# Weight conversion in two slots per half unit, and key sums ahead of the products that read them

## The chip, the cores and the metric

The kernel runs on one core of a Trainium2 chip. The metric is device time in microseconds (us), the median of several runs; lower is better. The engines are TensorE (PE, with PEld for its weight loads), VectorE (DVE), ScalarE (ACT), GpSimd (POOL) and SyncE (SP, which here issues every transfer). Each engine works through its own queue in order: an instruction that waits for another engine holds up everything behind it in its queue.

## The reference

Three layers are computed one after the other, all in float32 accuracy:

```
attention, per batch (4) and head (8), 576 positions, head size 64
    phi(x) = [exp(x w - m), exp(-(x w - m))],  m = max |x w|   (128 + 128 features)
    kv = phi(k)^T v,   z = sum phi(k)
    out = (phi(q) kv) / (phi(q) z + 1e-6)
layer 1 (2304 tokens, 512 -> 2048 -> 512):  h = x w_in;  y = (h cos h) w_out
layer 2: a gate over 8 experts (softmax, then 8 rounds of row and column scaling),
    out = sum over experts of P[:, e] * (relu(x w1[e]) w2[e])    (512 -> 1024 -> 512)
```

The weights of layer 1, `w_in` and `w_out`, are float64. The kernel reads them as pairs of 32-bit words and makes float32 values of them itself.

## The kernel before

Products that need full accuracy are split: a value becomes a rounded high part (made by ACT, `act_hi`) and the rest as a low part (`dve_lo` on DVE or `pool_lo` on POOL), and a product takes three matmuls (`mm3`).

**Attention.** The 4 batches and 8 heads are worked in 16 pairs of heads. `attention()` (L331) is a software pipeline over `i` with three pairs in work at once: pair `i` is loaded, turned and projected, pair `i-1` gets its key sums, query features and the final products, and pair `i-2` is written out as input of layer 1. The string `ORDER` (L478) says in which order these steps are written within an iteration: `t` turns (transposes) queries or keys into tile `pa` and splits them to `Th`, `Tl`; `r` does the same for the remainder (`tr` is the turn, plain `r` its projection); `p` projects to `pp`, and DVE centres the result (`m`, then `u`); `c` is one of four pieces of the key sums `pk`, after the last of which ACT copies `kvz`; `f` turns `u` of the queries to `pu` and ACT takes the exponentials `qp`; `g` multiplies `qp` with `kvz` to `pn`, and DVE divides (`rd`, `xn`); `x` turns `xn` to `px` and `pz` and splits it to `xh`, `xl`; `k` advances the weight conversion by one slot. The exponentials of the keys, `kp`, are deferred by `KD` steps. PSUM tiles of the stage come from one pool of seven buffers, so a `pp` or `pu` can only be written when the tile seven before it has been read by ACT or DVE.

**Conversion.** `convert(f)` (L109) makes unit `f` of the layer 1 weights (16 units of two halves, so 32 halves). A half takes three slots: load the raw words (`raw`); mask, clamp and shift the high word on DVE (three operations on `cmag`) and take the low word to `csgn` on ACT; then on DVE put the sign in (`csgn`), on POOL add (`cmag`), on ACT round (`csp`, high part), on POOL subtract (`csp`, low part), and store to `wd`.

**Who sets the order.** What is written is not yet what stands in the queues: a scheduler takes the instructions, with the written order as priority, and places each on its engine's queue when its own model holds the engine free and the inputs ready. It moves conversion slots forward as far as buffers allow. The queues are then fixed; on the chip nothing is reordered.

After attention come layer 1 (`moe1_steps`, four blocks of 512 tokens and a rest of 256) and layer 2 over two passes and eight experts. Neither is touched by the change.

Of the kernel before, what the change touches and what calls it, by code (L numbers as in the profile page):

```python
# [9 lines left out]
F32 = mybir.dt.float32  # L10
F32R = mybir.dt.float32r
I32 = mybir.dt.int32
U32 = mybir.dt.uint32
AF = mybir.ActivationFunctionType
ALU = mybir.AluOpType
# [10 lines left out]
def kernel(ctx: ExitStack, tc: tile.TileContext, q, k, v, w_phi,  # L26
                         moe_w_in, moe_w_out, moe2_w_gate, moe2_w1, moe2_w2, out):
    nc = tc.nc
    B, H, S, D = q.shape
    NT, DM = out.shape  # L30
    DFF = moe_w_out.shape[0]
    NE, _, DF2 = moe2_w1.shape
    P = 128
    NP = H // 2
    KC = DM // P
    NF1 = DFF // P
# [27 lines left out]
    def pool_lo(lo, raw, hi):  # L64
        nc.gpsimd.tensor_tensor(out=lo, in0=raw, in1=hi.bitcast(F32), op=ALU.subtract)  # L65
# [4 lines left out]
    def act_hi(hi, raw):  # L70
        nc.scalar.copy(out=hi, in_=raw)  # L71
# [25 lines left out]
    vpool = ectx.enter_context(tc.tile_pool(name="vpool", bufs=2))  # L97
    apool = actx.enter_context(tc.tile_pool(name="apool", bufs=2, side="right"))
# [6 lines left out]
    wd = [dpool.tile([P, 2, 2, DM], F32, name=f"wd{f}") for f in range(NF1)]  # L105
    win32 = moe_w_in.bitcast(I32)
    wout32 = moe_w_out.bitcast(I32)

    def convert(f):  # L109
        for i in range(2):  # L110
            raw = vpool.tile([P, DM, 2], I32, name="raw64")
            if i == 0:
                nc.sync.dma_start(out=raw.rearrange("p (k f) t -> p k (f t)", k=KC),
                                  in_=win32[:, f * 2 * P:(f + 1) * 2 * P].rearrange("(k p) f -> p k f", p=P))
            else:
                nc.sync.dma_start(out=raw.rearrange("p f t -> p (f t)"), in_=wout32[f * P:(f + 1) * P, :])
            yield
            hw = raw[:, :, 1]
            lw = raw[:, :, 0].bitcast(U32)
            mag = vpool.tile([P, DM], I32, name="cmag", bufs=CB)  # L120
            sgn = vpool.tile([P, DM], I32, name="csgn", bufs=CB)
            nc.vector.tensor_scalar(out=mag, in0=hw, scalar1=2 ** 31 - 1, scalar2=None, op0=ALU.bitwise_and)
            nc.vector.tensor_scalar(out=mag.bitcast(F32), in0=mag.bitcast(F32), scalar1=2.0 ** -15, scalar2=None, op0=ALU.max)
            nc.vector.tensor_scalar(out=mag, in0=mag, scalar1=3, scalar2=None, op0=ALU.logical_shift_left)
            nc.scalar.activation(out=sgn.bitcast(F32), in_=lw, func=AF.Copy, scale=2.0 ** -51, bias=2.0)
            yield
            nc.vector.scalar_tensor_tensor(out=sgn, in0=hw, scalar=-2 ** 31, in1=sgn, op0=ALU.bitwise_and, op1=ALU.bitwise_or)
            nc.gpsimd.tensor_tensor(out=mag, in0=mag, in1=sgn, op=ALU.add)  # L128
            res = mag.bitcast(F32)
            sp = vpool.tile([P, 2, DM], F32R, name="csp")  # L130
            act_hi(sp[:, 0, :], res)
            pool_lo(sp[:, 1, :], res, sp[:, 0, :])
            nc.sync.dma_start(out=wd[f][:, i, :, :], in_=sp.bitcast(F32))
            yield

    vx_t = []
# [49 lines left out]
    def defer(n, fn):  # L186
        late.append([n, fn])
# [47 lines left out]
    def project_rem(st):  # L235
# [7 lines left out]
        st["kp"][2] = t  # L243
        defer(KD, lambda: exps((t[:, 0, :], t[:, 1, :]), u[:, 0, :]))
        yield 0.44

    def project(st, s, unit):
# [6 lines left out]
        if s == 0:  # L254
            t = apool.tile([P, 4, 2, P], F32, name="kp4")
            st["kp"][unit] = t
            defer(KD, lambda: exps((t[:, :, 0, :], t[:, :, 1, :]), u))
        else:
# [28 lines left out]
    def attend(st, unit):  # L287
        pn = apsum("pn")
        kvz, qp = st["kvz"], st["qp"][unit]
        if unit == 2:  # L290
            st["xn"] = apool.tile([P, 5, 2, D], F32, name="xn", bufs=XB)
            for a in range(2):
                for s in range(2):
                    nc.tensor.matmul(pn[0:D, a * P:(a + 1) * P], qp[:, s, a * D:(a + 1) * D], kvz[:, a, s, :],  # L294
                                     start=(s == 0), stop=(s == 1))
            pv = pn[0:D, 0:2 * P].rearrange("p (a c) -> p a c", a=2)
            xo = st["xn"][0:D, 4, :, :]
            n, pr = 2, D
        else:
            for j in range(4):  # L300
                for s in range(2):
                    nc.tensor.matmul(pn[:, j * P:(j + 1) * P], qp[:, s, j * P:(j + 1) * P], kvz[:, unit, s, :],  # L302
                                     start=(s == 0), stop=(s == 1))
            pv = pn.rearrange("p (j c) -> p j c", j=4)
            xo = st["xn"][:, 0:4, unit, :]
            n, pr = 4, P
        r = apool.tile([P, 4], F32, name="rd", bufs=4)[0:pr, 0:n]
        nc.vector.tensor_scalar(out=r, in0=pv[:, :, D], scalar1=1e-6, scalar2=None, op0=ALU.add)
        nc.vector.reciprocal(r, r)
        nc.vector.tensor_tensor(out=xo, in0=pv[:, :, 0:D], in1=r.unsqueeze(2).to_broadcast([pr, n, D]), op=ALU.mult)  # L310
        yield 0.44 * n
# [19 lines left out]
    def attention():  # L331
        nxt = load_heads(0, 0)
        work = {}
        for i in range(B * NP + 2):
            work = {0: nxt, 1: work.get(0), 2: work.get(1)}
            sums = key_sums(work[1]) if work[1] else None
            for step in ORDER.split():
                kind, arg = step[0], step[1:]
                st = work[0 if kind in "tprL" else 2 if kind == "x" else 1]
                if kind == "k":  # L340
                    if i < B * NP:
                        next(conv, None)
                elif st is None:
                    continue
                elif kind == "L":
                    nxt = load_heads(*divmod(i + 1, NP)) if i + 1 < B * NP else None
                elif kind == "c":
                    yield next(sums)
                elif kind == "t":
                    yield from turn_heads(st, arg)  # L350
                elif kind == "f":
                    yield from query_features(st, int(arg))
                elif kind == "r":
                    yield from project_rem(st)
                elif kind == "p":
                    yield from project(st, int(arg) // 2, int(arg) % 2)
                elif kind == "g":
                    yield from attend(st, int(arg))
                else:
                    yield from emit_x(st)  # L360
# [114 lines left out]
        defer(1, turn_logits)  # L475

    LAG = 2
    ORDER = "t0 c0 k t1 c1 x tr f0 c2 k p0 c3 L f1 p1 f2 r p2 g2 k p3 g0 k g1"  # L478
    XB = 1
    UB = 4  # L480
    KD = 1
    LD = 1
    MD = 1
    GD = 3
    CB = 2
# [28 lines left out]
    def pair_tile(b):  # L514
        pool = xpool2 if b < B - 1 else xpool
        return tuple(pool.tile([P, KC, MAIN], F32R, name=f"{n}{b}", bufs=1) for n in ("xh", "xl"))

    def conversion():
        for f in range(NF1):
            yield from convert(f)  # L520
            done_conv[0] = f + 1

    done_conv = [0]
    conv = conversion()
# [272 lines left out]
```

## Time and profile before

| | us |
| --- | --- |
| median of 3 runs (lowest to highest) | 2261.55 (2259.89 to 2261.65) |
| the profiled execution | 2266.37 |
| its span | 2264.6 |
| PE busy in it | 2200.8 (97%) |
| DVE busy | 1334.0 (59%) |
| POOL busy | 1070.0 (47%) |
| ACT busy | 966.1 (43%) |

The median is what a change is measured by; the profiled execution is where durations and waits are read. Times of rows are counted from the start of the span. A share of the whole span mixes stages with different limits: attention runs to about 310 us, where the last `pn` is done, and everything behind it is layer 1 and layer 2.

### The profile page before, as it was taken

Reading aid. Unit: us, or ns where it says so; the run is one execution under the profiler, and the core shown is the slowest. Engines: PE = TensorE matmul, PEld = TensorE weight load, DVE = VectorE, ACT = ScalarE, POOL = GpSimd, SP = SyncE. Lnnn points to the kernel's source line nnn. Section 1 sums busy time; section 2 is a strip of 40 time slices with the busy share of each in tenths; the row PEclk is TensorE's granted clock in tenths of the full one; section 3 lists DMA queues with packets and bytes.
Section 4 is the critical chain, followed back from the end, with each engine's and each line's share of the span. In section 5 each row is a group of like instructions: output and inputs, shape, how many; then the busy total and the mean of one; then the engine's idle time right before and its main releaser. Section 6 shows DMA issues by size and latency. Waiting matters only on the chain.

```text
span 2264.6 us, 33017 instructions
## 1 busy us (share of the span) xinstructions
PE 2200.8 (97%) x12853; PEld 1955.6 (86%) x12853; DVE 1334.0 (59%) x2498; ACT 966.1 (43%) x1565; POOL 1070.0 (47%) x704
## 2 busy tenths in 40 slices
PE   7988999999999999999999999989999999999999
PEld 7878888778787888999999999979999999999998
DVE  6879753333553886555555555685555555555555
ACT  4555555445554433343433434443433333343332
POOL 3324210000000566666675766755766757667562
PEclk8989999999999999999999999999999999999999
DMA  5766325555543211111111111131111111111111
GB/s 174 223 209 203 115 75 189 198 189 189 185 147 119 66 46 39 47 47 47 45 41 47 47 47 47 41 98 47 47 47 47 39 46 47 47 47 48 38 37 43
DMA packets 130956, 198.31 MB, mean 88 GB/s; under 512 B 33136, under 2 KB 87536, under 8 KB 130800
## 3 DMA queue, kind: packets, MB, share of 16 engines
q1 hardware_dynamic: 130800, 196.20, 26.7%
q8 instruction: 101, 1.65, 0.3%
q14 instruction: 55, 0.45, 0.1%
HBM read 169.95 MB, written 26.21 MB: 87 GB/s over the span
## 4 chain that ended last, share of the span: by engine, by line
PE 87%; DVE 5%; ACT 2%; DMA 1%; issue 1%; POOL 1%; SPq 0%; DVEq 0%; ACTq 0%; POOLq 0%
PE py L91 33%; PE pm L91 30%; PE ph L377 8%; PE acc L423 7%; PE pn L302 2%; PE pk L272 1%; PE pp L91 1%; PE acc L416 1%; POOL cmag L128 1%; PE pn L294 1%; DVE xcl L68 1%; DMA xs<-x2d 1%; PE ph L463 1%; POOL csp L65 0%; DMA raw<-in_moe_w_in_dram 0%
## 5 line engine op out<-in xcount | busy, mean ns | idle before, releaser
L704 DVE SCALAR_TENSOR_TENSOR acc<-py,logit,acc 128x512 f32<-128x512 f32 x531 | 398.3, 751 | 352.6 <-PE py L91 352.6
L91 PE MATMUL pm<-xch,w1h 128*128 128x288 f32 x1792 | 531.6, 297 | 4.4 <-DVE r L658 3.1
L91 PE MATMUL pm<-xch,w1l 128*128 128x288 f32 x1792 | 531.3, 297 | 0.0
L91 PE MATMUL pm<-xcl,w1h 128*128 128x288 f32 x1792 | 523.6, 292 | 0.0
L91 PE MATMUL py<-w2h,hh 128*128 128x512 f32 x1152 | 451.6, 392 | 7.4 <-DVE acc L704 3.9
L91 PE MATMUL py<-w2l,hh 128*128 128x512 f32 x1152 | 452.2, 393 | 0.0
L91 PE MATMUL py<-w2h,hl 128*128 128x512 f32 x1152 | 452.0, 392 | 0.0
L65 POOL TENSOR_TENSOR hl<-r,hh 128x1152 fp32r<-128x1152 f32 x128 | 345.5, 2699 | 87.4 <-ACT hh L71 86.8
L65 POOL TENSOR_TENSOR w2l<-raw,w2h 128x1024 fp32r<-128x1024 f32 x64 | 155.6, 2432 | 415.7 <-DMA xs<-x2d 409.6
L91 PEld LDWEIGHTS pm<-xch,w1h 128*128 128x128 f32 x1792 | 337.1, 188 | 11.9 <-DVE r L658 4.2
L91 PEld LDWEIGHTS pm<-xcl,w1h 128*128 128x128 f32 x1792 | 341.7, 191 | 4.9
L91 PEld LDWEIGHTS pm<-xch,w1l 128*128 128x128 f32 x1792 | 336.6, 188 | 0.1
L600 POOL TENSOR_TENSOR w1l<-raw,w1h 128x256 fp32r<-128x256 f32 x124 | 90.6, 752 | 438.3 <-ACT w1h L71 429.4
L678 ACT ACTIVATE r<-r 128x1152 f32<-128x1152 f32 x128 | 149.1, 1165 | 267.6 <-DVE r L658 255.2
L91 PEld LDWEIGHTS py<-w2h,hh 128*128 128x128 f32 x1152 | 217.2, 189 | 52.5 <-DVE acc L704 5.8
L91 PEld LDWEIGHTS py<-w2h,hl 128*128 128x128 f32 x1152 | 217.2, 189 | 46.3 <-POOL hl L65 0.3
L91 PEld LDWEIGHTS py<-w2l,hh 128*128 128x128 f32 x1152 | 217.3, 189 | 42.4
L654 ACT COPY keep<-pm 128x288 f32<-128x288 f32 x256 | 101.5, 398 | 338.4 <-PE pm L91 332.8
L658 DVE TENSOR_TENSOR r<-r,pm 128x288 f32<-128x288 f32 x512 | 215.9, 452 | 41.2 <-PE pm L91 40.9
L600 POOL TENSOR_TENSOR w1l<-ssum,w1h 128x1280 fp32r<-128x1280 f32 x62 | 183.9, 2966 | 2.7 <-ACT w1h L71 0.7
L658 DVE TENSOR_TENSOR r<-keep,pm 128x288 f32<-128x288 f32 x128 | 58.1, 454 | 202.6 <-PE pm L91 200.4
L377 PE MATMUL ph<-xh,wsp 128*128 128x512 f32 x512 | 171.8, 397 | 1.7 <-ACT hh L71 0.8
(163 smaller groups left out, 3311.4 us busy)
## 6 DMA issues: line engine op xcount, KB each, us to landing
wsp<-wd SPq DMA_DIRECT2D x128, 512.0 KB, 4.6
raw<-in_moe_w_dram SPq DMA_DIRECT2D x128, 512.0 KB, 3.5
wd<-csp SPq DMA_DIRECT2D x32, 512.0 KB, 3.3
raw<-in_moe_w_in_dram SPq DMA_DIRECT2D x16, 512.0 KB, 5.1
raw<-in_moe_w_out_dram SPq DMA_DIRECT2D x16, 512.0 KB, 5.1
kraw<-in_k_dram SPq DMA_DIRECT2D x16, 256.0 KB, 4.0
qraw<-in_q_dram SPq DMA_DIRECT2D x16, 256.0 KB, 3.1
vx<-in_v_dram SPq DMA_DIRECT2D x32, 128.0 KB, 2.8
```

The source lines that it names most:

```text
L65: nc.gpsimd.tensor_tensor(out=lo, in0=raw, in1=hi.bitcast(F32), op=ALU.subtract)
L68: nc.vector.tensor_tensor(out=lo, in0=raw, in1=hi.bitcast(F32), op=ALU.subtract)
L91: nc.tensor.matmul(ps, a, b, start=(i == 0), stop=(i == len(ops) - 1))
L128: nc.gpsimd.tensor_tensor(out=mag, in0=mag, in1=sgn, op=ALU.add)
L302: nc.tensor.matmul(pn[:, j * P:(j + 1) * P], qp[:, s, j * P:(j + 1) * P], kvz[:, unit, s, :], start=(s == 0), stop=(s == 1))
L377: nc.tensor.matmul(ph[:, 0:n], w, x, start=(i == 0), stop=(i == len(ops) - 1))
L423: nc.tensor.matmul(accs[blk][d], w[:, ds], g, start=(f == 0 and i == 0), stop=(f == NF1 - 1 and i == 2))
L600: eng.tensor_tensor(out=lo[:, sl], in0=src, in1=hi[:, sl].bitcast(F32), op=ALU.subtract)
L654: nc.scalar.copy(out=t, in_=ps[m])
L658: nc.vector.tensor_tensor(out=r[:, u, th, :], in0=r[:, u, th, :] if a is None else ps[a], in1=ps[b], op=op)
L678: nc.scalar.activation(out=rf, in_=rf, func=AF.Relu)
L704: nc.vector.scalar_tensor_tensor(out=a, in0=py, scalar=pe, in1=a, op0=ALU.mult, op1=ALU.add)
```

## The change

The conversion of a half takes two slots where it took three, and the slots of neighbouring halves overlap: in one slot ACT rounds the half before (`act_hi`), the next raw words are fetched, and DVE and ACT start on the present half; in the other slot DVE puts the sign in, POOL subtracts for the half before and adds for the present one, and the half before is stored. The string `ORDER` puts all four pieces of the key sums to the front of an iteration, projects between them and the products that read them, puts `g0` first among these and has three `k` steps where it had four; the first iteration has none. `KD` goes from 1 to 2, and the tile `xn` is taken at the first `attend` of a pair, whichever that is.

```diff
-    def convert(f):
-        for i in range(2):
-            raw = vpool.tile([P, DM, 2], I32, name="raw64")
...
+    def conversion():
+        n = 2 * NF1
+        raws, mags, sps = {}, {}, {}
+        def fetch(h):
...
+        fetch(0)
+        yield
+        for h in range(n + 1):
+            if h > 0:
+                sps[h - 1] = vpool.tile([P, 2, DM], F32R, name="csp")
+                act_hi(sps[h - 1][:, 0, :], mags[h - 1].bitcast(F32))
+            if h < n:
+                if h + 1 < n:
+                    fetch(h + 1)
+                hw = raws[h][:, :, 1]
...
+                nc.scalar.activation(out=sgn.bitcast(F32), in_=raws[h][:, :, 0].bitcast(U32), func=AF.Copy,
+                                     scale=2.0 ** -51, bias=2.0)
+                nc.vector.tensor_scalar(out=mag, in0=hw, scalar1=2 ** 31 - 1, scalar2=None, op0=ALU.bitwise_and)
+                nc.vector.tensor_scalar(out=mag.bitcast(F32), in0=mag.bitcast(F32), scalar1=2.0 ** -15, scalar2=None, op0=ALU.max)
+                nc.vector.tensor_scalar(out=mag, in0=mag, scalar1=3, scalar2=None, op0=ALU.logical_shift_left)
+                mags[h] = mag
             yield
...
-            nc.vector.scalar_tensor_tensor(out=sgn, in0=hw, scalar=-2 ** 31, in1=sgn, op0=ALU.bitwise_and, op1=ALU.bitwise_or)
-            nc.gpsimd.tensor_tensor(out=mag, in0=mag, in1=sgn, op=ALU.add)
-            res = mag.bitcast(F32)
-            sp = vpool.tile([P, 2, DM], F32R, name="csp")
-            act_hi(sp[:, 0, :], res)
-            pool_lo(sp[:, 1, :], res, sp[:, 0, :])
-            nc.sync.dma_start(out=wd[f][:, i, :, :], in_=sp.bitcast(F32))
+            if h < n:
+                nc.vector.scalar_tensor_tensor(out=sgn, in0=hw, scalar=-2 ** 31, in1=sgn, op0=ALU.bitwise_and, op1=ALU.bitwise_or)
+            if h > 0:
+                sp = sps.pop(h - 1)
+                pool_lo(sp[:, 1, :], mags.pop(h - 1).bitcast(F32), sp[:, 0, :])
+                nc.sync.dma_start(out=wd[(h - 1) // 2][:, (h - 1) % 2, :, :], in_=sp.bitcast(F32))
+                done_conv[0] = h // 2
+            if h < n:
+                nc.gpsimd.tensor_tensor(out=mag, in0=mag, in1=sgn, op=ALU.add)
             yield
@@ attend
+        if "xn" not in st:
+            st["xn"] = apool.tile([P, 5, 2, D], F32, name="xn", bufs=XB)
         if unit == 2:
-            st["xn"] = apool.tile([P, 5, 2, D], F32, name="xn", bufs=XB)
@@ attention
-                    if i < B * NP:
+                    if 0 < i < B * NP:
                         next(conv, None)
@@
-    ORDER = "t0 c0 k t1 c1 x tr f0 c2 k p0 c3 L f1 p1 f2 r p2 g2 k p3 g0 k g1"
+    ORDER = "t0 c0 k c1 t1 c2 k x c3 tr f0 f2 p0 L f1 p1 r p2 g0 p3 g2 g1 k"
-    KD = 1
+    KD = 2
```

What stands in the queues shows the change better than the written order. Line numbers of the changed kernel differ (there, L135 to L150 are the conversion, L249 and L250 the exponentials, L291 is `kvz`, L226 `Tr`). The first place is ACT's queue around the copy `kvz_2309` of one and the same pair of heads (the eleventh). Before:

```order
L71 CAST csp_3800<-cmag_3778 128x512
L125 ACTIVATE csgn_3930<-raw64_3900 128x512
L71 CAST csp_3882<-cmag_3847 128x512
L274 COPY kvz_2309<-pk_2310 128x512
L232 ACTIVATE qp4_2404<-pu_2399 128x512
L232 ACTIVATE kp4_2378<-u_2374 128x4x128
L233 ACTIVATE kp4_2378<-u_2374 128x4x128
L233 ACTIVATE qp4_2404<-pu_2399 128x512
L232 ACTIVATE qp1_2423<-pu_2421 128x128
L233 ACTIVATE qp1_2423<-pu_2421 128x128
```

Now:

```order
L71 CAST csp_3651<-cmag_3600 128x512
L71 CAST Th_2325<-pa_2327 128x512
L135 ACTIVATE csgn_3656<-raw64_3598 128x512
L71 CAST xh2_2137<-px_2349 128x512
L71 CAST x4h_120<-pz_2355 128x64
L291 COPY kvz_2309<-pk_2310 128x512
L226 COPY Tr_2366<-pr_2367 128x256
L249 ACTIVATE qp4_2376<-pu_2371 128x512
L250 ACTIVATE qp4_2376<-pu_2371 128x512
L249 ACTIVATE qp1_2381<-pu_2379 128x128
L250 ACTIVATE qp1_2381<-pu_2379 128x128
```

The rounding `csp` that stood right ahead of `kvz` now stands further up, ahead of a turn and of `xh`; the exponentials of the keys (`kp`) no longer stand between those of the queries (`qp`).

The second place is PE's queue at the start of the third iteration, from the turn of the keys on. Before:

```order
L218 MATMUL pa<-ident,kraw 128x128 x4
L270 MATMUL pk<-vx_115,kp_383 128x128
L272 MATMUL pk<-vx_115,kp_328 128x128 x4
L218 MATMUL pa<-ident,qraw 128x128 x4
L270 MATMUL pk<-vx_115,kp_383 128x128
L272 MATMUL pk<-vx_115,kp_328 128x128 x4
L319 MATMUL px<-ident,xn 128x128 x4
L324 MATMUL pz<-ident,xn 128x64
L208 MATMUL pr<-ident,kraw 128x128
L208 MATMUL pr<-ident,qraw 128x128
L281 MATMUL pu<-ident,u 128x128 x4
L270 MATMUL pk<-vx_115,kp_383 128x128
```

Now:

```order
L235 MATMUL pa<-ident,kraw 128x128 x4
L287 MATMUL pk<-vx_115,kp_363 128x128
L289 MATMUL pk<-vx_115,kp_321 128x128 x4
L287 MATMUL pk<-vx_115,kp_363 128x128
L289 MATMUL pk<-vx_115,kp_321 128x128 x4
L235 MATMUL pa<-ident,qraw 128x128 x4
L287 MATMUL pk<-vx_115,kp_363 128x128
L289 MATMUL pk<-vx_115,kp_355 128x128 x4
L337 MATMUL px<-ident,xn 128x128 x4
L342 MATMUL pz<-ident,xn 128x64
L287 MATMUL pk<-vx_115,kp_363 128x128
L289 MATMUL pk<-vx_115,kp_355 128x128 x4
```

The key sums are complete at the twelfth row, where before their third piece only begins. Between their last matmul and the first `pn` stood 19 matmuls (four `pu`, six `pp`, one `pu`, eight `pp`); now 31 stand there.

The third place is DVE's queue at the start of the program, from the first turned keys on. Before:

```order
L68 TENSOR_TENSOR Tl_147<-pa_148,Th_146 128x512
L122 TENSOR_SCALAR cmag_171<-raw64_155 128x512
L68 TENSOR_TENSOR Tl_158<-pa_159,Th_157 128x512
L123 TENSOR_SCALAR cmag_171<-cmag_171 128x512
L228 TENSOR_REDUCE m_185<-pp_177 128x4
L124 TENSOR_SCALAR cmag_171<-cmag_171 128x512
L229 TENSOR_TENSOR u_184<-pp_177,m_185 128x512
```

Now:

```order
L68 TENSOR_TENSOR Tl_147<-pa_148,Th_146 128x512
L68 TENSOR_TENSOR Tl_156<-pa_157,Th_155 128x512
L245 TENSOR_REDUCE m_177<-pp_169 128x4
L245 TENSOR_REDUCE m_201<-pp_193 128x4
L246 TENSOR_TENSOR u_176<-pp_169,m_177 128x512
L246 TENSOR_TENSOR u_200<-pp_193,m_201 128x512
L245 TENSOR_REDUCE m_211<-pp_207 128x2
```

The conversion's first operation, which needs the raw words of the weights, no longer stands between the two `Tl`.

## Rows read from the trace of the kernel before

**Rows 1.** Page, busy times of the engines, and DVE in 40 slices

```profile
PE 2200.8 (97%) x12853; PEld 1955.6 (86%) x12853; DVE 1334.0 (59%) x2498; ACT 966.1 (43%) x1565; POOL 1070.0 (47%) x704
DVE  6879753333553886555555555685555555555555
```

**Rows 2.** Windows: stretch, length, busy PE, PEld, DVE, ACT, POOL, clock, DMA share, GB/s

```profile
32.19:243.46 211.27, 182.03 (x1452) 174.68 (x1453) 178.06 (x366) 117.13 (x256) 72.89 (x56) 0.94 0.66 210
70.87:88.43 17.56, 15.48 (x132) 14.87 (x132) 15.80 (x34) 10.90 (x25) 7.68 (x6) 1.00 0.73 214
223.53:243.46 19.93, 17.06 (x132) 16.45 (x133) 17.42 (x36) 11.24 (x25) 7.77 (x6) 0.91 0.64 203
275.44:291.41 15.97, 15.48 (x132) 14.87 (x132) 9.96 (x24) 7.62 (x20) 0.00 (x0) 1.00 0.01 2
291.41:304.84 13.43, 13.24 (x106) 12.09 (x107) 5.48 (x16) 5.25 (x14) 0.00 (x0) 1.00 0.00 0
```

**Rows 3.** Waits of PE over the span; the last row from 259.45 to 291.41

```profile
PE pn L294 <- ACT qp L232: 30.5, 15, 3.9
PE pp L91 <- DVE Tl L68: 3.3, 1, 3.3
PE pk L270 <- ACT kp L232: 1.6, 1, 1.6
...
PE pn L294 <- ACT qp L232: 1.0, 2, 0.5
```

**Rows 4.** Timeline: start, length, instruction, idle before; ACT and PE ahead of `pn`

```profile
220.19 0.62 ACT L71 CAST csp<-cmag 128x512 fp32r<-128x512 f32 x1 [1.16 <-POOL cmag L128]
220.71 0.58 ACT L274 COPY kvz<-pk 128x512 f32<-128x512 f32 x1
221.68 0.63 ACT L232 ACTIVATE kp<-u 128x512 f32<-128x512 f32 x1
222.20 0.63 ACT L233 ACTIVATE kp<-u 128x512 f32<-128x512 f32 x1
223.19 0.28 ACT L232 ACTIVATE qp<-pu 128x128 f32<-128x128 f32 x1
...
223.53 0.98 PE L294 MATMUL pn<-kvz,qp 128*64 128x128 f32 x7 [2.85 <-ACT qp L232]
```

**Rows 5.** Timeline of POOL and DVE in the same microseconds

```profile
218.88 1.27 POOL L128 TENSOR_TENSOR cmag<-cmag,csgn 128x512 int32<-128x512 int32 x1 [0.37 <-DVE cmag L124]
220.88 1.27 POOL L65 TENSOR_TENSOR csp<-cmag,csp 128x512 fp32r<-128x512 f32 x1 [0.73 <-ACT csp L71]
...
219.32 1.12 DVE L122 TENSOR_SCALAR cmag<-raw 128x512 int32<-128x512 int32 x1
220.96 1.47 DVE L123 TENSOR_SCALAR cmag<-cmag 128x512 f32<-128x512 f32 x1
```

**Rows 6.** Groups by line, 0 to 304: count, busy, mean ns, idle before, releasers

```profile
L128 POOL TENSOR_TENSOR cmag<-cmag,csgn 128x512 int32<-128x512 int32 x32 | 42.0, 1312 | 136.5 <-DVE cmag L124 68.2 <-DVE rd L309 38.6 <-DVE csgn L127 18.8
...
L127 DVE SCALAR_TENSOR_TENSOR csgn<-raw,csgn 128x512 int32<-128x512 int32 x32 | 27.5, 861 | 0.0
...
L123 DVE TENSOR_SCALAR cmag<-cmag 128x512 f32<-128x512 f32 x32 | 24.9, 780 | 0.2
...
L124 DVE TENSOR_SCALAR cmag<-cmag 128x512 int32<-128x512 int32 x32 | 19.9, 623 | 0.2
...
L122 DVE TENSOR_SCALAR cmag<-raw 128x512 int32<-128x512 int32 x32 | 18.5, 579 | 8.0 <-DMA raw<-in_moe_w_in_dram 8.0
```

**Rows 7.** Timeline of the program's start: DVE, then PE

```profile
13.20 0.43 DVE L122 TENSOR_SCALAR cmag<-raw 128x512 int32<-128x512 int32 x1 [6.17 <-DMA raw<-in_moe_w_in_dram]
14.14 0.42 DVE L123 TENSOR_SCALAR cmag<-cmag 128x512 f32<-128x512 f32 x1
18.46 0.68 DVE L127 SCALAR_TENSOR_TENSOR csgn<-raw,csgn 128x512 int32<-128x512 int32 x1
...
20.55 0.77 PE L270 MATMUL pk<-vx,kp 128*128 128x128 f32 x2 [1.64 <-ACT kp L232]
```

More of the change, by code (lines that the diff above doesn't have):

```diff
@@ L107 @@
     wout32 = moe_w_out.bitcast(I32)
-    def convert(f):
-        for i in range(2):
+    def conversion():
+        n = 2 * NF1
+        raws, mags, sps = {}, {}, {}
+        def fetch(h):
+            f, i = divmod(h, 2)
             raw = vpool.tile([P, DM, 2], I32, name="raw64")
@@ L116, in convert @@
                 nc.sync.dma_start(out=raw.rearrange("p f t -> p (f t)"), in_=wout32[f * P:(f + 1) * P, :])
-            yield
[L118 to L123, printed above, removed]
@@ L124, in convert @@
-            nc.vector.tensor_scalar(out=mag, in0=mag, scalar1=3, scalar2=None, op0=ALU.logical_shift_left)
-            nc.scalar.activation(out=sgn.bitcast(F32), in_=lw, func=AF.Copy, scale=2.0 ** -51, bias=2.0)
-            yield
-            nc.vector.scalar_tensor_tensor(out=sgn, in0=hw, scalar=-2 ** 31, in1=sgn, op0=ALU.bitwise_and, op1=ALU.bitwise_or)
-            nc.gpsimd.tensor_tensor(out=mag, in0=mag, in1=sgn, op=ALU.add)
-            res = mag.bitcast(F32)
-            sp = vpool.tile([P, 2, DM], F32R, name="csp")
@@ L131, in convert @@
-            act_hi(sp[:, 0, :], res)
-            pool_lo(sp[:, 1, :], res, sp[:, 0, :])
-            nc.sync.dma_start(out=wd[f][:, i, :, :], in_=sp.bitcast(F32))
+            raws[h] = raw
+        fetch(0)
[8 more added lines that the diff above has]
+                hw = raws[h][:, :, 1]
+                mag = vpool.tile([P, DM], I32, name="cmag", bufs=CB)
+                sgn = vpool.tile([P, DM], I32, name="csgn", bufs=CB)
+                nc.scalar.activation(out=sgn.bitcast(F32), in_=raws[h][:, :, 0].bitcast(U32), func=AF.Copy,
[4 more added lines that the diff above has]
+                mags[h] = mag
+            yield
+            if h < n:
[7 more added lines that the diff above has]
+                nc.gpsimd.tensor_tensor(out=mag, in0=mag, in1=sgn, op=ALU.add)
@@ L516, in pair_tile @@
         return tuple(pool.tile([P, KC, MAIN], F32R, name=f"{n}{b}", bufs=1) for n in ("xh", "xl"))
[L518 to L521, printed above, removed]
     done_conv = [0]
```

## The prediction

> **What bounds the kernel now.** I read the page's busy times first: PE is busy for 2200.8 of 2264.6 us [rows 1], so all its idle time is 64 us, and nothing that this change touches can be worth more than the part of it that lies in attention, plus time in which PE ran at its lower clock there. Next the waits of PE over the whole span [rows 3]: one dominates, `pn` waiting for the exponentials `qp` of the queries on ACT, 15 times and 30.5 us. The other two of interest happen once each at the program's start, 3.3 us for `Tl` and 1.6 us for `kp`. Third the windows, cut at the first `pn` of an iteration [rows 2]. From 32.19 to 243.46 eleven iterations take 211.27 us, 19.2 each, and in them the conversion runs (DVE holds 366 instructions, where eleven iterations without conversion would hold 264). From 275.44 an iteration without conversion takes 15.97, of which PE is busy 15.48. So attention is bound by PE only where there is no conversion; where there is, an iteration loses 3.3 us.
>
> What causes the loss is read from one such place, fourth view: `pn` starts at 223.53 after 2.85 us of waiting [rows 4]. Back from it in ACT's queue: `qp` at 223.19, two `kp`, `kvz` at 220.71, and `csp` at 220.19, which stood 1.16 us for the addition `cmag` on POOL. That addition ran from 218.88 to 220.15 and had itself waited for DVE [rows 5]. So PE waits for a chain DVE, POOL, ACT that belongs to the weights, with the keys' exponentials thrown in. It also costs clock: in the iteration that ends with this wait the granted clock is 0.91 and the same 132 or 133 matmuls are busy for 17.06 us, against 15.48 at 1.00 [rows 2].
>
> The fifth view is DVE, since it is what remains when the chain is loosened. Its busy time per iteration is 9.96 us without conversion and 178.06/11 = 16.2 with it [rows 2], a little above PE's 15.48. The reason is in the groups by line [rows 6]: the four conversion operations take 27.5 + 24.9 + 19.9 + 18.5 = 90.8 us for 32 halves, 0.71 each, while at the program's start, before POOL has any of this work, they take 0.43, 0.42 and 0.68 [rows 7]; with 0.42 for the third `cmag` operation 32 halves would take 62 us. The 29 us between are stretching beside POOL: the operation at 220.96 lasts 1.47 instead of 0.42, while POOL runs its subtraction from 220.88 to 222.15 [rows 5].
>
> **The change, part by part.** *The written order and KD.* Nothing is computed more or less; matmuls, DVE, ACT and POOL operations are the same in number. PE's queue has 31 instead of 19 matmuls between the last key sum and the first `pn`, and ACT's has `kvz`, `Tr` and one pair of exponentials ahead of what that `pn` needs, instead of `kvz` and three pairs. That takes away the remaining wait of the iterations without conversion, 0.5 us each [rows 3]. `kp` comes later, but is first used in the next iteration; from `kvz` on ACT has about 0.6 + 0.4 + 4 x 0.6 + 4 x 0.6 + a few of 0.3, some 7 us, and PE at least 9 us of products in that time, so it is hidden. Two such iterations: -1.0. The last interval, 13.43 with PE busy 13.24 [rows 2], gives -0.2. The earlier allocation of `xn` costs nothing: its writer follows the transposes `px` of the former tile on PE.
>
> *The two slots.* `csp` now rounds a half whose addition was issued a slot before, and stands away from `kvz`. It still waits for POOL when it comes too early, and then in front of `Th` or `xh`; behind `xh` is DVE's `xl`, which frees a PSUM tile that the second projection of the iteration needs. A delay of 1 to 2 us there is mostly covered by the 31 matmuls in front of the first `pn`. What stays is throughput. DVE keeps 128 conversion operations; the first iteration now has none, so they spread over about twelve intervals instead of eleven: some 118 / 12 = 9.8 in each, at 0.67 as in [rows 2] ((178.06 - 11 x 9.96) / 102), so 9.96 + 6.6 = 16.5 us of DVE per interval. DVE isn't busy all the time: 84% over the eleven intervals, but 15.80 of 17.56, 90%, in the one from 70.87 where PE waited little. With the chain loosened I take 94%, a little above that: 16.5/0.94 = 17.6 us per interval. Twelve of them are 211.2. Before, the same twelve are 211.27 and one free interval of 16.0, 227.3. So -16.1. Bounds: below, PE's own 15.48, which is -41.5; above, the chain remains in another form and twelve intervals take 19.2, which is +3.1. Neither the stretching at a denser POOL nor the covered part is shown in any row; my value lies near the busy time of DVE because that is the row nearest to what is left.
>
> *The transfers.* Loads of raw words are issued a slot earlier, but into the same two buffers, which DVE's sign operation frees, so they land hardly earlier; DVE's own waits for them are 8.0 us in all and 6.17 of that is one wait at the start [rows 6, 7]. Stores and the loads of `k`, `q`, `v` share SP's queue in nearly the old order. I count zero, with one us either way.
>
> *The start.* DVE stood 6.17 us for the first raw words [rows 7] with the second `Tl` behind it, and PE 3.3 us for that `Tl` [rows 3]. Now no conversion stands there, so `Tl` follows 5 us earlier, and `u` and `kp` behind it. The first key sum started at 20.55 [rows 7]. What is late next are the second pair's loads, which move forward by one transfer of about 0.6 us only, and ACT's `kp`. Bounds 0 and -6; I take -4, the wait of 3.3 and part of the 1.6.
>
> The sum is -16.1 - 1.0 - 0.2 - 4 = -21.3 us, all in the first 310 us; the queues behind are the same, and layer 1 and 2 leave PE hardly any idle time, so nothing gives it back. Against the profiled execution that is 2266.4 (span 2264.6 and 1.8 around it) - 21.3 = 2245.1. That execution lies 4.8 above the median of the runs, so the median should come to 2261.55 - 21.3 = 2240.2, rounded 2240.
>
> The page "SBUF — State Buffer" of the Trainium skill, section "Who interferes with whom", speaks against the change: a VectorE operation in a two-port mode or with two SBUF inputs and a GpSimd operation exclude each other for the whole instruction. The trace agrees as far as [rows 5] go: the stretched operation ended just after POOL's. By that rule every microsecond in which POOL is packed closer is one in which the conversion's DVE operations stand; it makes the third rival below more likely, and the sum above takes the stretch as it was.
>
> **The rivals.** *First, PE becomes the bound.* If the conversion operations meet POOL less often, DVE needs 9.96 + 9.8 x 0.48 = 14.7 us per interval, less than PE's 15.48, and the intervals come to about 16. Then 12 x 16 = 192, -35, and with the other terms 2221. For it: POOL's two operations of neighbouring halves can now run together, and at clock 1.00 PE's time is stable. Against it: POOL does the same 64 operations of 1.3 us, 83 us, in less time.
>
> *Second, it doesn't do what it says.* `csp` still waits for an addition of the same iteration, only in front of other work, and intervals stay at 18.9 to 19.6: -0.5 to +8 on the twelve, with the start and the free intervals -6 to +3, so about 2259 in the middle. For it: POOL's queue still alternates addition and subtraction, and in the ACT rows shown with the change a `csp` stands ahead of `xh`.
>
> *Third, slower: DVE stands for POOL.* If POOL no longer pauses between a subtraction and the next addition (before there was 0.37 us, and 0.73 for ACT in the other order [rows 5]), a DVE operation caught at the front may stand for both, 2.6 us instead of 1.3. The stretch per operation would go from 0.67 - 0.48 = 0.19 to 0.38: DVE 9.96 + 9.8 x 0.86 = 18.4 us per interval, 19.6 at 94%, and more where `xl` and `u`, queued behind, free PSUM late. At 20 the twelve take 240, +12.7, and 2262 - 5 + 13 = 2269. It decides from 19.4 us per interval on, where the gain of start and free intervals (5.2) is eaten.
>
> **How the numbers follow.** Forecast 0.62 (intervals 16.6 to 18.9, times 2228 to 2256); first rival 0.12 (2208 to 2228); second 0.16 (2255 to 2264); third 0.10 (2262 to 2275). The forecast's own range is that of its intervals: 16.5, DVE never idle, gives 12 x 16.6 = 199 and -28 - 5; 18.9 gives -0.5 - 5. The range of 8 in 10 takes this with a little of the neighbours: 2226 to 2257. About 0.2%, 4.5 us, is what a measurement of this kernel can tell from no change. Faster by more than that (below 2257): the forecast, the first rival and a third of the second, 0.79. Within: the rest of the second and a part of the third, 0.12. Slower: 0.09.
>
> **What would show it.** Right: in the new profile PE's wait of `pn` for `qp` falls from 30.5 to under 8 us; the conversion intervals are 16.6 to 18.9 long with DVE busy above 90% of them; the first key sum starts near 16 to 17 instead of 20.55; free intervals take 15.5; the clock between 32 and 243 is above 0.94; behind the end of attention everything has the length it had. Wrong: a new wait of PE of more than 15 us in sum (for `xl`, `u` or `Th`) while DVE is below 85%, which would be the second rival; mean times of the four conversion operations above 0.85 with DVE near full, the third; DVE's means near 0.5 and PE without waits, the first; or a later part of the program, layer 1's first block above all, that takes longer than before.

## The result, and the profile after

| us | before | after |
| --- | --- | --- |
| median (lowest to highest), 4 runs each | 2261.6 (2259.89 to 2262.53) | 2234.32 (2233.70 to 2236.09) |
| the profiled execution, its span | 2266.37, 2264.6 | 2234.69, 2232.9 |

The ratio is 0.9882, with a 95% interval of 0.9864 to 0.9899: 27.3 us less, where 21.3 were forecast. The page's busy times and the two slices rows that answer to [rows 1]:

```profile
PE 2192.2 (98%) x12853; PEld 1946.3 (87%) x12853; DVE 1325.6 (59%) x2498; ACT 962.8 (43%) x1565; POOL 1070.4 (48%) x704
DVE  7998643334555985555555555675555555555555
PEclk9999999999999999999999999999999999999999
```

The counts of instructions are the same. DVE's first slices are denser, and the work of attention ends earlier. The waits of PE over the span (us in total, times, longest), against [rows 3]:

```profile
PE pp L91 <- DVE xl L68: 12.3, 7, 3.0
...
PE pp L255 <- ACT Tr L226: 1.8, 2, 1.2
...
PE pu L298 <- DVE Tl L68: 0.7, 2, 0.4
```

The wait of `pn` for `qp`, 30.5 us before, no longer stands in this list, nor do the single waits for `Tl` of `pp` and for `kp` at the start. A smaller one has come: the second projection `pp` waits for `xl`, whose reading frees a PSUM tile. For the windows I now cut at the turn of the keys, which starts an iteration in both kernels. Of before, the second iteration and the twelve behind it (columns as in [rows 2]):

```profile
16.58:37.60 21.02, 18.94 (x129) 18.19 (x129) 14.81 (x32) 11.35 (x26) 5.34 (x4) 0.76 0.57 182
37.60:264.86 227.26, 197.53 (x1587) 189.57 (x1586) 190.47 (x396) 125.83 (x275) 77.99 (x60) 0.94 0.64 202
```

And of after: the same iteration, then of the twelve a slow one, two quicker ones and a slow one, the first iteration behind them, which holds only the end of the conversion (one addition and one subtraction on POOL), and the twelve together:

```profile
13.50:28.75 15.25, 15.06 (x129) 14.38 (x128) 12.47 (x25) 10.24 (x25) 5.10 (x4) 1.00 0.75 227
28.75:50.49 21.74, 19.14 (x135) 17.80 (x133) 16.27 (x41) 10.86 (x25) 5.08 (x4) 0.84 0.77 231
82.89:100.15 17.26, 15.73 (x134) 14.95 (x133) 16.67 (x37) 10.38 (x24) 7.83 (x6) 1.00 0.73 241
171.09:186.55 15.46, 15.46 (x135) 14.92 (x134) 11.20 (x29) 8.71 (x20) 2.55 (x2) 1.00 0.69 206
202.01:222.90 20.89, 17.49 (x134) 16.51 (x133) 18.74 (x39) 11.50 (x25) 7.64 (x6) 0.92 0.78 255
238.69:254.14 15.45, 15.45 (x134) 14.91 (x133) 10.53 (x28) 8.23 (x19) 2.55 (x2) 1.00 0.19 54
28.75:238.69 209.94, 194.97 (x1587) 185.46 (x1586) 187.21 (x400) 123.25 (x276) 74.60 (x58) 0.97 0.71 221
```

The twelve are uneven: they take from 15.46 us, with 29 instructions on DVE, to 21.74, with 41. The length of a window less PE's busy time is PE's idle time. Busy time that changes at an equal number of matmuls is mostly clock; a few tenths of a microsecond per iteration are not (at 1.00 throughout, 134 matmuls are busy for 15.45 us in one row and for 15.73 in another). So the program is 37.60 - 28.75 = 8.85 us ahead when the twelve begin and gains 17.32 in them (17.5 each, was 18.9): 14.76 of it idle time (29.73 to 14.97) and 2.56 busy time, where the granted clock rose from 0.94 to 0.97. The free iterations and the last interval give 1.9 more: `px` of the last pair comes at 282.9 instead of 311.0, 28.1 us earlier. Behind attention the two profiled executions differ by another 3.6. The medians differ by 27.3 only, and the profiled execution of before lies 4.8 above its median, so nothing shows these 3.6 to come from the change.

Where the new wait comes from is read from one place, the iteration that starts at 202.01 (start, length, instruction, idle before):

```profile
206.23 0.60 PE L337 MATMUL px<-ident,xn 128*128 128x128 f32 x4
...
207.40 0.58 ACT L71 CAST Th<-pa 128x512 fp32r<-128x512 f32 x1
207.57 1.28 POOL L65 TENSOR_TENSOR csp<-cmag,csp 128x512 fp32r<-128x512 f32 x1 [0.73 <-ACT csp L71]
207.65 1.49 DVE L138 TENSOR_SCALAR cmag<-cmag 128x512 f32<-128x512 f32 x1
...
209.68 1.26 POOL L150 TENSOR_TENSOR cmag<-cmag,csgn 128x512 int32<-128x512 int32 x1 [0.83 <-DVE cmag L139]
...
210.98 0.62 ACT L71 CAST csp<-cmag 128x512 fp32r<-128x512 f32 x1 [3.00 <-POOL cmag L150]
...
211.50 0.58 ACT L71 CAST xh<-px 128x512 fp32r<-128x512 f32 x1
211.67 1.27 POOL L65 TENSOR_TENSOR csp<-cmag,csp 128x512 fp32r<-128x512 f32 x1 [0.73 <-ACT csp L71]
211.72 1.50 DVE L139 TENSOR_SCALAR cmag<-cmag 128x512 int32<-128x512 int32 x1
...
213.15 0.68 DVE L68 TENSOR_TENSOR xl<-px,xh 128x512 fp32r<-128x512 f32 x1
...
213.88 0.39 PE L91 MATMUL pp<-wblkh,Th 128*128 128x256 f32 x1 [2.97 <-DVE xl L68]
```

`px` is done at 206.8, and ACT is free at 207.98, yet `xh` starts at 211.50: `csp` stands ahead of it in ACT's queue, 3.00 us for POOL's addition. Then `xl` is ready to go at 212.08 and starts at 213.15, since DVE is in a conversion operation of 1.50 us, stretched from 0.43 while POOL runs. The addition that `csp` waits for had itself waited 0.83 us for DVE's `cmag`, so the old chain DVE, POOL, ACT is still there, in front of other work. At this place both neighbours delay `xl`, ACT's wait by some three us and DVE's queue by one.

The conversion's operations, 0 to 300, against [rows 6]:

```profile
L143 DVE SCALAR_TENSOR_TENSOR csgn<-raw,csgn 128x512 int32<-128x512 int32 x32 | 27.9, 871 | 3.1 <-ACT csgn L135 3.1
L139 DVE TENSOR_SCALAR cmag<-cmag 128x512 int32<-128x512 int32 x32 | 23.9, 747 | 0.4
L137 DVE TENSOR_SCALAR cmag<-raw 128x512 int32<-128x512 int32 x32 | 21.6, 674 | 6.7 <-DMA raw<-in_moe_w_in_dram 4.6 <-DMA raw<-in_moe_w_out_dram 2.0
L138 DVE TENSOR_SCALAR cmag<-cmag 128x512 f32<-128x512 f32 x32 | 17.8, 555 | 0.4
```

They sum to 91.2 us, before 90.8: the stretch beside POOL is neither better nor worse.

### The profile page after: what moved, and what is told of

The parts are those of the page before. It is cut to its first block, busy times and chain, and to the rows that moved or that the text cites. A ratio compares the mean times of both kernels' runs of the same rounds, so it can differ in the third digit from the quotient of the medians.

```text
span 2232.9 us, 33061 instructions
## 1 busy us (share of the span) xinstructions
PE 2192.2 (98%) x12853; PEld 1946.3 (87%) x12853; DVE 1325.6 (59%) x2498; ACT 962.8 (43%) x1565; POOL 1070.4 (48%) x704
## 4 chain that ended last, share of the span: by engine, by line
PE 89%; DVE 4%; issue 2%; POOL 1%; DMA 1%; ACT 1%; SPq 0%; DVEq 0%; POOLq 0%; ACTq 0%
PE py L91 34%; PE pm L91 31%; PE ph L395 9%; PE acc L441 8%; PE pn L320 2%; PE pk L289 1%; PE pp L91 1%; PE acc L434 1%; DVE xcl L68 1%; PE ph L481 1%; POOL cmag L150 1%; POOL csp L65 1%; PE pn L312 0%; DVE csgn L143 0%; PE pk L287 0%
```

## The experiments

Ratios are to the kernel before on the same chip. The table holds the twelve iterations of each kernel (the same 1586 or 1587 matmuls), in us: where they start and end, PE's idle time and clock in them, DVE's busy time.

| kernel | ratio (95%) | start, end | length | PE idle | clock | DVE busy |
| --- | --- | --- | --- | --- | --- | --- |
| before | 1 | 37.60, 264.86 | 227.26 | 29.73 | 0.94 | 190.47 |
| after | 0.9882 (0.9864 to 0.9899) | 28.75, 238.69 | 209.94 | 14.97 | 0.97 | 187.21 |
| e1_conv_only | 0.9935 (0.9917 to 0.9953) | 37.42, 251.43 | 214.01 | 21.81 | 0.97 | 180.27 |
| e2_order_only | 0.9866 (0.9851 to 0.9881) | 28.69, 234.61 | 205.92 | 15.72 | 0.98 | 180.32 |
| e3_conv_at_start | 0.9864 (0.9848 to 0.9881) | 35.30, 233.94 | 198.64 | 9.16 | 0.99 | 180.15 |
| e4_skip_only | 1.0010 (1.0001 to 1.0020) | 33.81, 265.64 | 231.83 | 32.78 | 0.93 | 189.63 |
| e10_order_string | 0.9880 (0.9859 to 0.9900) | 35.57, 236.20 | 200.63 | 10.64 | 0.99 | 176.15 |
| e6_small_pool | 0.9785 (0.9763 to 0.9807) | 30.07, 218.81 | 188.74 | 1.87 | 1.00 | 157.71 |
| e8_round_late | 0.9861 (0.9841 to 0.9881) | 28.98, 235.21 | 206.23 | 14.10 | 0.98 | 187.03 |
| e9_no_max | 0.9824 (0.9798 to 0.9851) | 30.36, 224.36 | 194.00 | 6.04 | 1.00 | 161.88 |
| e7_x_early | 0.9871 (0.9848 to 0.9893) | 28.73, 230.38 | 201.65 | 13.52 | 1.00 | 178.98 |
| e11_act_abs | 0.9861 (0.9845 to 0.9878) | 36.19, 231.66 | 195.47 | 7.26 | 1.00 | 159.22 |
| e12_old_conv_act_abs | 0.9908 (0.9892 to 0.9923) | 35.18, 241.22 | 206.04 | 16.31 | 0.99 | 166.17 |
| e13_act_abs_x_early | 0.9848 (0.9833 to 0.9863) | 37.23, 230.37 | 193.14 | 5.95 | 1.00 | 158.55 |

### Which part of the change does it

**The two slots alone** (after, with the old string, the old `KD` and conversion in the first iteration).

```diff
-                    if 0 < i < B * NP:
+                    if i < B * NP:
-    ORDER = "t0 c0 k c1 t1 c2 k x c3 tr f0 f2 p0 L f1 p1 r p2 g0 p3 g2 g1 k"
-    KD = 2
+    ORDER = "t0 c0 k t1 c1 x tr f0 c2 k p0 c3 L f1 p1 f2 r p2 g2 k p3 g0 k g1"
+    KD = 1
```

> The conversion in two overlapping slots alone, with the old written order, KD = 1 and conversion in the first iteration too. Theory (the gain has three parts: about 9 us at the start because no conversion stands there, about 17 us over the twelve conversion iterations, of which the order of PE's and ACT's work is the larger share, and 0.5 to 2 us later): the exponentials of the keys still stand between kvz and the first pn, so PE's wait of pn for qp stays above 15 us, and the time is 2250 to 2258, 4 to 12 us below the kernel before. Rival (the overlapped slots do the work, since they take the POOL chain out of ACT's queue): 2236 to 2246, and the wait of pn for qp below 10 us.

Measured: 2247.65 against 2260.25, 12.6 us less, between the ranges of the two theories. The wait that the two slots were to loosen is mostly still there:

```profile
PE pn L312 <- ACT qp L249: 24.9, 15, 3.6
```

It is 5.6 us shorter than before. The twelve end 13.43 earlier; PE's idle time in them falls by 7.92 and its busy time by 5.33, at a clock of 0.97. So with the old order the two slots are worth something.

**Order, KD and the free first iteration, with the old conversion** (before, with the string, `KD` and first iteration of after and its `xn`; that is after with the old `convert` in three slots).

```diff
-                    if i < B * NP:
+                    if 0 < i < B * NP:
...
-    ORDER = "t0 c0 k t1 c1 x tr f0 c2 k p0 c3 L f1 p1 f2 r p2 g2 k p3 g0 k g1"
+    ORDER = "t0 c0 k c1 t1 c2 k x c3 tr f0 f2 p0 L f1 p1 r p2 g0 p3 g2 g1 k"
...
-    KD = 1
+    KD = 2
```

> The new written order, KD = 2, the earlier xn tile and no conversion in the first iteration, with the old conversion in three slots. Theory: the start is as in the changed kernel (third turn of keys near 29 us) and the wait of pn for qp is below 8 us; the rounding that waits for POOL now stands in front of other work; time 2236 to 2246, most of the gain. Rival (the overlapped slots do the work): 2250 to 2258.

Measured: 2230.83 against 2260.25, 29.4 less, below even the range that said most of the gain, and PE's list has no wait of `pn` for `qp`. The whole gain is there without the two slots.

**The first iteration's part, from both sides**: before without conversion in the first iteration, and after with it.

```diff
(e4_skip_only, from before)
-                    if i < B * NP:
+                    if 0 < i < B * NP:
(e3_conv_at_start, from after)
-                    if 0 < i < B * NP:
+                    if i < B * NP:
```

> The kernel before, only without conversion slots in the first iteration. Theory: about 6 to 9 us of the start come with this one condition: 2252 to 2256, with the third turn of keys near 29 to 31 us instead of 37.6. Rival (conversion starts later, so one more of the slow iterations follows at the end, and the gain is given back): 2258 to 2263.

> The changed kernel, only with conversion slots in the first iteration again. Theory: the start is worth about 9 us, of which 3 are the wait for the first raw words and the rest waits and the lower clock of the second iteration that follow from it; the second turn of keys is late again (16 to 17 us instead of 13.5), the third near 33 to 38, and the time is 2239 to 2244. Rival (the start was only shifted: conversion that begins earlier also ends earlier, and gives the time back in the iterations): 2232 to 2237.

Measured: 2263.67 against 2260.25 for the one, slower by 0.1% with an interval that only just leaves out no change, and 2230.19 against 2260.25, 30.1 less, for the other. Both speak for the rival, that the start was only shifted, though the first lies just above the rival's range and the second just below; the second's ratio cannot be told from that of after. The windows show what becomes of the start, first of before without conversion there, then of after with it:

```profile
12.71:33.81 21.10, 16.94 (x129) 15.96 (x128) 14.29 (x33) 10.44 (x25) 2.55 (x2) 0.92 0.71 217
33.81:265.64 231.83, 199.05 (x1586) 191.12 (x1585) 189.63 (x397) 127.10 (x277) 80.87 (x62) 0.93 0.63 199
```

```profile
16.45:35.30 18.85, 17.00 (x128) 16.48 (x128) 17.86 (x34) 11.21 (x26) 5.63 (x5) 0.88 0.62 190
35.30:233.94 198.64, 189.48 (x1586) 180.97 (x1585) 180.15 (x393) 123.11 (x274) 77.95 (x60) 0.99 0.74 230
```

The first gains 3.8 us until the twelve begin and loses 4.6 in them. The second begins them 6.55 us later than after, and then takes 16.55 an iteration instead of 17.5, and ends them 4.75 earlier. What the conversion leaves undone in the first iteration it does later, at the same price or more. That shows the start to be no gain of its own.

**The string alone** (before, with the new string; `xn` taken at the first `attend`, which that string needs).

```diff
+        if "xn" not in st:
+            st["xn"] = apool.tile([P, 5, 2, D], F32, name="xn", bufs=XB)
         if unit == 2:
-            st["xn"] = apool.tile([P, 5, 2, D], F32, name="xn", bufs=XB)
...
-    ORDER = "t0 c0 k t1 c1 x tr f0 c2 k p0 c3 L f1 p1 f2 r p2 g2 k p3 g0 k g1"
+    ORDER = "t0 c0 k c1 t1 c2 k x c3 tr f0 f2 p0 L f1 p1 r p2 g0 p3 g2 g1 k"
```

> The kernel before with the new string ORDER (and the earlier xn tile it needs) alone: old conversion, KD = 1, conversion in the first iteration. Theory (the place of the key sums ahead of the products is the whole gain; the two slots, KD and the start add nothing to it): 2226 to 2233, wait of pn for qp below 5 us. Rival (KD = 2, which takes the keys' exponentials out of the way of the queries', is needed too): 2237 to 2248, wait of pn for qp above 10 us.

Measured: 2235.65 against 2262.95, 27.3 less, the same as the whole change, though between the ranges of the two theories. `pn` no longer waits for `qp`, though conversion, `KD` and the first iteration are those of before; over the span, the largest waits of PE in attention, beside those of the start, are

```profile
PE pp L91 <- DVE xl L68: 5.4, 4, 3.0
PE pp L238 <- ACT Tr L209: 4.8, 3, 1.8
```

and its busy time in the twelve falls from 197.53 to 189.99. So of the 26.6 us that they gain 19.1 are idle time and 7.5 busy time, where the clock rose from 0.94 to 0.99. The string makes several moves at once (key sums to the front, other work ahead of the first `pn`, `g0` first, three `k` where there were four); no run takes them apart.

### What sets the intervals then

**POOL almost out of it** (after; POOL adds 8 of 512 columns and doesn't subtract, the high part is stored in both places).

```diff
-                pool_lo(sp[:, 1, :], mags.pop(h - 1).bitcast(F32), sp[:, 0, :])
...
-                nc.gpsimd.tensor_tensor(out=mag, in0=mag, in1=sgn, op=ALU.add)
+                nc.gpsimd.tensor_tensor(out=mag[:, 0:8], in0=mag[:, 0:8], in1=sgn[:, 0:8], op=ALU.add)
```

> The changed kernel with POOL's part of the conversion cut to next to nothing: the addition runs on 8 of 512 columns, the subtraction is left out and the high part is stored in its place too (two stores of half the size). DVE and ACT keep all their operations. Theory (what still makes the conversion iterations longer than 15.5 us is POOL: DVE's operations stretched beside it, and ACT's rounding waiting for it): the four DVE operations fall to about 0.42, 0.42, 0.42 and 0.68 us, 62 us in all, PE's wait for xl to below 4 us, and the time is 2212 to 2222. Rival (the number of DVE operations and the loads of raw words set the length): 2228 to 2236, wait for xl still above 8 us.

Measured: 2214.05 against 2262.95, 48.9 less, as the theory had it; `pp` no longer waits for `xl`. DVE's conversion groups, same view as above:

```profile
L143 DVE SCALAR_TENSOR_TENSOR csgn<-raw,csgn 128x512 int32<-128x512 int32 x32 | 21.7, 678 | 2.0 <-ACT csgn L135 2.0
...
L138 DVE TENSOR_SCALAR cmag<-cmag 128x512 f32<-128x512 f32 x32 | 13.5, 422 | 0.3
```

All four come to 62.1 us instead of 91.2, what [rows 7] give for operations without POOL. The twelve take 15.7 each with PE idle for 1.87 us in all: without POOL's work PE is the bound. The edit changes two things at once: it takes the stretch on DVE away, and it cuts the time that ACT stands for POOL, from 46.5 us in after to 21.1.

**One DVE operation less** (after without the clamp).

```diff
-                nc.vector.tensor_scalar(out=mag.bitcast(F32), in0=mag.bitcast(F32), scalar1=2.0 ** -15, scalar2=None, op0=ALU.max)
```

> The changed kernel with one of the four DVE operations of a half left out (the clamp of the high word), which takes 17.8 us out of DVE's queue and leaves POOL and ACT alone. Theory 2 (DVE's throughput): 2222 to 2230, PE's wait for xl below 7 us. Theory 1 (ACT standing for POOL): 2231 to 2236, wait for xl above 9 us.

Measured: 2222.08 against 2262.95, 40.9 less, in the range of the theory that DVE's throughput decides, and so is PE's wait for `xl`:

```profile
PE pp L91 <- DVE xl L68: 5.9, 8, 1.6
```

The operation held DVE for 17.8 us; the end of the twelve comes 14.3 earlier than in after. The twelve are 15.9 shorter, of which 8.9 are idle time of PE and 7.0 busy time, at a clock of 1.00 instead of 0.97. This speaks for DVE's work, but it is no proof: the edit also shortens the chain to POOL, and ACT's waits for POOL's addition fall from 46.5 to 38.8.

**The rounding a slot later** (after; `act_hi` behind the next half's DVE operations, POOL's subtraction a round later, three buffers).

```diff
+            if 0 < h <= n:
+                sps[h - 1] = vpool.tile([P, 2, DM], F32R, name="csp")
+                act_hi(sps[h - 1][:, 0, :], mags[h - 1].bitcast(F32))
...
-    CB = 2
+    CB = 3
```

> The changed kernel with ACT's rounding one slot later and the low part one more (three cmag buffers), so that rounding follows its addition by a whole slot; work and stretching beside POOL unchanged. Theory 1 (ACT standing for POOL in front of xh is what delays xl and so PE): ACT's wait for the addition falls from 46 to below 15 us, PE's wait for xl from 12.3 to below 4, time 2221 to 2229. Theory 2 (DVE's own queue, stretched beside POOL, delays xl): wait for xl stays above 8 us, time 2231 to 2239.

Measured: 2231.56 against 2262.95, 31.4 less, which cannot be told from after. The wait that it was to take away stayed (23 waits of ACT's `csp` and 43.9 us, in after 24 and 46.5; PE's for `xl` 11.8 and 12.3): from 101.00 here and from 104.25 in after ACT's queue has the same order, `csp`, `Th`, `csp`, `xh`, `x4h`, `csgn`, `kvz`. The scheduler, which moves conversion work forward, seems to have put the rounding back. So it doesn't test the theory, and whether `xl` is late in sum by ACT's wait or by DVE's queue stays open.

### Can more be had

**`x` earlier in the string** (after).

```diff
-    ORDER = "t0 c0 k c1 t1 c2 k x c3 tr f0 f2 p0 L f1 p1 r p2 g0 p3 g2 g1 k"
+    ORDER = "t0 c0 k c1 x t1 c2 k c3 tr f0 f2 p0 L f1 p1 r p2 g0 p3 g2 g1 k"
```

> The changed kernel with the turn x and the later pieces of the key sums in another order: t0 c0 k c1 x t1 c2 k c3, so that px is turned one key-sum piece and one turn earlier. Theory (what PE still waits for, xl behind xh, is a matter of how late xh is asked for): wait for xl below 7 us instead of 12.3, time 2227 to 2232. Rival (DVE's and POOL's amount of work sets the iterations, so a wait taken away here comes back elsewhere): 2232 to 2238.

Measured: 2230.18 against 2258.96, 28.8 less; not told from after. The time is the theory's, but what happens is the rival's: PE's wait for `xl` is gone and others have its place:

```profile
PE px L337 <- DVE xn L328: 8.1, 9, 1.5
...
PE pp L255 <- ACT Tr L226: 5.0, 4, 1.6
```

**A DVE operation moved to ACT**: the mask becomes an absolute value on ACT, in after with conversion at the start, in the string alone, and in the first of these with `x` earlier.

```diff
-                nc.vector.tensor_scalar(out=mag, in0=hw, scalar1=2 ** 31 - 1, scalar2=None, op0=ALU.bitwise_and)
+                nc.scalar.activation(out=mag.bitcast(F32), in_=hw.bitcast(F32), func=AF.Abs)
```

> The changed kernel with conversion in the first iteration again, and the mask of the high word taken from DVE to ACT (Abs in place of the bitwise and), nothing left out. Theory (DVE's amount of work, with its stretching, is what makes the conversion iterations longer than 15.5 us, while ACT has room): DVE's conversion falls by 18 to 22 us, and the time is 2217 to 2226, 5 to 13 us below the same kernel without this step. Rival (ACT's queue, with 32 more operations of about 0.6 us ahead of Th and xh, takes the place of DVE's): 2229 to 2238.

> The kernel before with the new string ORDER, KD = 1, the old conversion in three slots, and the mask of the high word on ACT. Theory (order plus less work on DVE is all that counts, the two slots nothing): within 4 us of the run with the new conversion and the same mask on ACT, 2218 to 2229. Rival (the two slots help once DVE has room): 5 us or more above it.

> The mask on ACT, conversion in the first iteration, and x one piece earlier, together. If both waits are separate, 3 to 5 us below the kernel with the mask on ACT alone, 2213 to 2222; if the intervals are already at PE's 15.5, no difference within 2 us.

Measured, all against 2258.96: 2227.68, 2239.36 and 2225.34. The first takes 21 us of work from DVE and gains nothing that can be told from 0.9864 without it (e3), where 5 to 13 us were expected: DVE now stands for ACT (`csgn` 14.4 us in 8 waits). In the second DVE stands longer, and PE with it:

```profile
DVE cmag L123 <- ACT cmag L122: 24.2, 12, 5.0
PE pp L91 <- DVE xl L68: 17.9, 9, 3.2
```

Between the first two lies only the change but for its string (two slots, `KD`), and here the two differ: 0.9861 against 0.9908, intervals that don't meet. That a conversion without the overlap of halves is held up by one more step between ACT and DVE is the likely reason; no run keeps `KD` and changes only the slots here. The third, 0.9848, is the lowest of the kernels that leave nothing out; its interval (0.9833 to 0.9863) ends below that of after by 0.0001 only.

## Why the prediction was right, and where it was not

The number was right in part by luck: of its terms one was right by errors that cancel, one was less than half of what the windows show, and the gain was put down to a part of the change that is not needed for it.

*The twelve intervals: right in length, by errors that cancel.* 17.5 each against 17.6, and 17.3 us gained against 16.1; `pn` no longer waits, the clock from 28.75 to 238.69 is 0.97, the stretch is unchanged as assumed. But I took 16.5 us of DVE at 94%, and it is 187.21/12 = 15.6 at 89%, under the 90% that I had named as a sign of being right. The price of 0.67 an operation came from a wrong count: I took what [rows 2] hold above 24 instructions an iteration, 102, but the lines of the same window, 32.19 to 243.46 of before, hold 115:

```profile
L127 DVE SCALAR_TENSOR_TENSOR csgn<-raw,csgn 128x512 int32<-128x512 int32 x29 | 25.5, 880 | 0.0
L123 DVE TENSOR_SCALAR cmag<-cmag 128x512 f32<-128x512 f32 x29 | 23.2, 801 | 0.2
L124 DVE TENSOR_SCALAR cmag<-cmag 128x512 int32<-128x512 int32 x28 | 18.3, 653 | 0.2
L122 DVE TENSOR_SCALAR cmag<-raw 128x512 int32<-128x512 int32 x29 | 17.2, 591 | 1.8 <-DMA raw<-in_moe_w_in_dram 1.8
```

So over a free iteration an operation cost (178.06 - 109.56)/115 = 0.60 us. After, the twelve hold 119, where I had 118, at (187.21 - 119.5)/119 = 0.57. With 0.60 my own sum would have been 15.8/0.94 = 16.9 us an interval and -25 for the twelve; the share of 94%, too high, took that back. That DVE's work decides is supported by e9 and e6; that it can fill 94% is not: in every kernel whose `pn` doesn't wait and whose conversion is whole on DVE and POOL its share lies between 88% and 91%. I also put the clock of 0.91 to the iteration that ends with the wait; the row from 223.53 is the one that begins behind it.

*The start: mis-sized, and wrong in its meaning.* I predicted -4 from waits; the trace shows -8.85. That lies outside my bounds of 0 and -6. 4.97 of it come mostly from waits, near what I took: 3.08 are gained up to the second pair's turn of the keys (16.58 to 13.50), where the wait of 3.3 for `Tl` is gone, and 1.89 are PE's idle time in the iteration behind (2.08 to 0.19). The other 3.88 is clock, which I did not price: the same 129 matmuls take 15.06 us at 1.00 instead of 18.94 at 0.76. The first key sum, at 20.55 before [rows 7] and forecast for 16 to 17, shows it too: it comes earlier, and its two matmuls take 0.46 us instead of 0.77:

```profile
15.24 0.46 PE L287 MATMUL pk<-vx,kp 128*128 128x128 f32 x2
```

But I added it as a gain of its own, and e4 and e3 show that it is none: the conversion left out there makes the intervals behind it longer. The step that failed is the -4 of the start as a term beside the twelve: both hang together through one stock of conversion work.

*The two slots: credited with what the order did.* My part on them held that the chain DVE, POOL, ACT had to be loosened for `pn` to stop waiting. The string alone does that (e10, -27.3), and I had given the order only -1.2. Its 31 instead of 19 matmuls behind the key sums are the likely reason, but its moves were not run one by one. The two slots alone leave 24.9 us of the wait (e1, -12.6) and add nothing measurable to the new order (after against e2). They are a help of their own with the old order, and perhaps with more work on ACT (e12 against e11, where `KD` differs too). Nor is the delay of `xl` mostly covered by the matmuls in front of `pn`, as I had it: PE waits 12.3 us for it. The sum was right and its attribution was not.

*Free iterations and the last interval: right.* 15.45 instead of 15.98, with all PE's time filled; 1.9 us against 1.2.

*Transfers and the rest: right in attention.* No new wait for a transfer stands on PE's list; of the 3.6 us behind attention no run shows that they belong to the change.

*The rivals.* PE as the bound over all twelve was seen only where POOL's work was left out (e6, 15.7 an interval, and its DVE means of 0.42 and 0.68); in after single iterations reach it, as the one from 171.09. The second rival's mechanism is there, `csp` waiting 46.5 us for POOL (37.7 before), at times in front of `xh`, but PE's wait for `xl` is 12.3 us where 30.5 went, which stays under the 15 that I had set, and DVE is at 89%, above my 85%. Of the third nothing is seen: the mean of the four operations is 0.71 as before.

## What to carry to other kernels

When a chain of background work delays the work on the critical engine, first move the consumer further from the chain; a few independent products put between producer and consumer did here what restructuring the chain alone did not. Background work with a fixed total is one stock: leaving it out at the start put it where it hurt as much later, so price the whole stretch in which it is done, not its start. And where waits go, count the clock too, from windows with equal numbers of matmuls.

## What was not expected of the hardware

The clock is a large term beside the waits: in the second iteration PE's busy time for 129 matmuls was 18.94 us at a mean granted clock of 0.76 where PE had waited 3.3 us for `Tl` just before it and waited 1.6 for `kp` in it, and 15.06 at 1.00 without these waits. And the price of POOL's work on DVE could be measured whole: 128 operations take 62.1 us when POOL is almost idle and 91.2 beside its 64 operations, 0.23 each on the mean, with single ones going from 0.43 to 1.50. The operations with an operand in PSUM show no such stretch: in the changed kernel the 64 `u` take 0.67 to 0.69 us each and the 16 `xl` 0.68 to 0.69.
